# Three pairs' sums in attention and earlier slot conversions in a fused attention, MoE and gated-MLP kernel

## Chip, cores and metric

One Trainium2 chip, one core. The metric is the device time of one execution in microseconds (us), median of three runs; smaller is better.

## What is computed

```python
# q, k, v: [4, 8, 576, 64]; x: [2304, 512]; 8 experts 512 -> 1024 -> 512; then 512 -> 2048 -> 512, all float32
proj = x @ w_phi; proj -= max(abs(proj)); phi = concat(exp(proj), exp(-proj))
kv = sum_s phi(k) v;  z = sum_s phi(k)
attn = (phi(q) kv) / (phi(q) z + 1e-6)
# top-1 mixture of experts on the rows of attn
e = argmax(softmax(cosine(x, emb) / tau));  x = gate * (relu(x @ w1[e]) @ w2[e])
# gated layer
h = x @ w_in;  out = (h * sigmoid(h)) @ w_out
```

Every product is kept near float32 by splitting both operands into a high part (a rounded copy) and a low part (the rest) and adding three products: high by high, high by low and low by high. `w_in` and `w_out` arrive as 64-bit floats and are narrowed to 32 bits on the chip by integer operations.

## The kernel before

The order of work on every engine is the order of the program text; the engines run it in order, and an instruction that waits holds up all that stands behind it on its engine. So does the SyncE queue for DMAs and GpSimd's queue for its own DMAs and gathers.

**Attention** (0 to about 245 us). A loop over g = -2 to 31, one head of one batch each, about 6.5 us apiece. VectorE finds the maxima and subtracts them (L383, L384), ScalarE takes exponentials, GpSimd makes the low parts (`klow` L422, `low` L369), TensorE does the rest. Beside it, class `Convert` narrows 10 of the 16 blocks of `w_in`, numbers 4 to 13, two to a pair (pairs 2 to 6). One block costs four VectorE instructions (`narrow`: L194, L187 or L190, L199, L201). The dictionaries `CONV` and `BITS` say in which g a block is begun and two of its instructions run. Pairs 2 and 3 live in a region of eight 256-column pieces each; `SUMS` says in which g their sums are made (`sums`, L180 and twice L183: the gated layer's first product is done by a seven-product Strassen scheme, whose left operands are three plain pieces and four sums), after which one DMA stores pieces 1 to 7 in `sscr`. Of the other pairs only the four plain pieces are stored.

**Slots** (about 231 to 527 us). 22 slots of 128 tokens, each with one expert. In turn s of the loop TensorE does the first product of slot s in four blocks (`mm1(s, k)`, k = 0 to 3), transposes the rows of slot s+1 (`xturn`), does the second product of slot s-1 in four blocks (`mm2(s-1, i)`) and transposes the hidden rows of slot s (`hturn`). Behind `mm1(s, k)` ScalarE rounds a quarter of the next slot's weights into `wh` (L835) and VectorE makes the low part `wl` (L836); behind `mm2(s-1, i)` the same is done for the second weights of slot s. `xturn` ends with `xh` on ScalarE (L840) and `xl` on VectorE (L843), `hturn` with `hh` and `hl` on the same lines. In slots 1 to 8 VectorE also does the routing of the remaining slots in 13 bits (`route`, `PLAN`); the bit with the gate (L703) comes behind `mm1(4, 1)`, and ScalarE's L705 waits for it.

In the same loop six more blocks of `w_in` (J0 to J5) are narrowed in place, in a tile `x` of attention. `convert(s, n)` is called behind `mm1(s, n)` for n = 0 to 3 and behind `mm2(s-1, n-4)` for n = 4 to 7. `STEPS` lists the (s, n) at which one of the four parts of a block runs: part 1 on VectorE (L187 or L190), part 2 on VectorE (L209), part 3 on ScalarE (L212), part 4 on VectorE (L215). Each waits for the one before. `SLOTWORK` lists GpSimd's share: `cload` loads a raw block, `cplain` stores a narrowed one, `csum` and `cstore` make and store sums.

**Gated layer, first part** (about 524 to 711 us). 32 units of seven products each, about 0.8 us a product; unit u = 8k + q is token part k against pair q. `unit` runs the products in the order 1 of u, 5 of u, 4 of u-1, 6 of u, 3 of u-1, 2 of u, 7 of u. Behind products 1, 4, 6 and 7 ScalarE copies out (`keep`, L1110); behind 1, 3 and 2 VectorE joins (`join`, L1117), and SyncE stores the result. The join behind product 1 has to be done before product 3 of the same unit can write its bank. `at(u, n, f)` puts further work behind product n of unit u, in the order in which the text puts it there: weights (`wfetch`, `wsum`, `whigh`, `wlow`), inputs of the next part (`xsum`, `xsplit`), and the narrowing of `w_out`: `oload(j)` (SyncE, 512 KB), four times `owork(j)` (VectorE L194, L190, L199, L201), `ostore(j)` (SyncE). `oload` uses two buffers in turn, shared with `wfetch`.

```python
            for j, u in enumerate(units):
                at(u - 1, 4, oload, j)
            for j, u in enumerate(units):
                for n in (3, 3, 2, 2):
                    at(u, n, owork, j)
                at(u, 7, ostore, j)
```

**Gated layer, second part** (about 711 us to the end): 18 row tiles, TensorE throughout.

Of the kernel before, what the change touches and what calls it, by code (L numbers as in the profile page):

```python
# [12 lines left out]
I32 = mybir.dt.int32  # L13
# [21 lines left out]
NJP = NJ // 2  # L35
# [8 lines left out]
KWHOLE = 26  # L44
CA = 10
CT = 4
QD = 4
G = B * H
RK = 2
NXS = (2, 2, 2)  # L50
SQ = [{}, {1: (0, 1), 3: (2, 3), 5: (4,)}, {1: (0, 1), 3: (2, 3), 5: (4,)}, {i: (i,) for i in range(NB)}]
RANK = (1, 0)
WARM = (10, 14)
SUMS = {3: 0, 5: 0, 6: 0, 12: 1, 19: 1, 20: 1}
BITS = [-1, 0, 1, 2, 3, 4, 5, 6, 7, 11, 12, 13, 14, 15, 19, 20, 21, 22, 23, 24]
CONV = [-2, 0, 2, 4, 6, 11, 13, 15, 20, 22, 24]
ORDERED = {ET.PE, ET.Activation, ET.DVE, ET.SP}
# [12 lines left out]
def moe_kernel(ctx, tc, qk, v, w_phi, emb, tau, w1, w2, win, wout, out):  # L70
    nc = tc.nc
# [107 lines left out]
    def sums(r, eng):  # L179
        eng.tensor_tensor(out=r[:, 4:8:3], in0=r[:, 1:3], in1=r[:, 0:1].to_broadcast([P, 2, 256]), op=ALU.add)  # L180
        yield
        for o in (5, 6):
            eng.tensor_tensor(out=r[:, o], in0=r[:, o - 1], in1=r[:, o - 3], op=ALU.add)  # L183
# [33 lines left out]
    class Convert:  # L217
        def __init__(self, a, b):
            self.a, self.b, self.h, self.s = a, b, {}, {}

        def done(self, i):
            p, even = divmod(i, 2)
            o = 512 * (1 - even)
            return (self.b[:, p * 2048 + o:p * 2048 + o + 512] if p < 2 else self.a[:, 3072 + o:3584 + o]).bitcast(I32)

        def load(self, i):
            o = i % 3 * 1024
# [1 line left out]
            fetch_raw(i + CT, self.h[i])  # L229

        def step(self, k):
            if k > 4:
                keep_weights(k - 1 + CT, self.done(k - 1))
            if k + 2 < CA:
                self.load(k + 2)
            if k < CA:
                yield from narrow(self.h.pop(k), self.done(k), k)

        def pair(self, p):
            r = self.b[:, p * 2048:(p + 1) * 2048].rearrange("p (a f) -> p a f", a=8)  # L240
            yield from sums(r, nc.vector)
            yield
            nc.sync.dma_start(out=sscr[CT // 2 + p], in_=r[:, 1:8])

    def phase_all(ctx):
        x_ctx = ExitStack()
# [697 lines left out]
        def cplain(i):  # L944
            keep_weights(i + NJ - 2, J[i][0][:, 0:512], nc.gpsimd)

        SLOTWORK = {(3, 1): (cplain, 0), (4, 1): (cload, 2), (8, 3): (cplain, 1), (8, 7): (cload, 3),
                    (11, 1): (csum, 1), (13, 1): (cstore, 1), (13, 5): (cload, 4), (13, 7): (cload, 5),
                    (16, 1): (csum, 2), (16, 3): (cstore, 2)}
        STEPS = [(2, 1), (2, 3), (2, 5), (2, 7), (7, 1), (7, 5), (7, 7), (8, 1)]  # L950
        STEPS += [(s, n) for s in (9, 10, 14, 15) for n in (1, 3, 5, 7)]

        def convert(s, n):
# [13 lines left out]
        W = {}  # L967
# [14 lines left out]

        def wfetch(q):
            if q < QD:
                wspace(q)
                nc.sync.dma_start(out=W[q][1].bitcast(F32), in_=sscr[q].rearrange("p a f -> p (a f)"))
            else:
                W["r", q] = pools["ul"].tile([P, 2048], F32, tag="ws", name="ws", bufs=2)
                nc.sync.dma_start(out=W["r", q][:, 0:1024], in_=sscr[q].rearrange("p a f -> p (a f)"))
# [292 lines left out]
        project(1)  # L1282
        next(prep)
        cv = Convert(*(raw2[i].rearrange("p k f -> p (k f)") for i in (1, 0)))
        pairs = [cv.pair(p) for p in range(2)]
        first = None
        ch = [iter(())]
        cg = [iter(())]
# [9 lines left out]
        for g in range(-2, G):  # L1298
            b, h = divmod(g, H)
            for u in (3, 4) if g == -2 else (g + 6,):  # L1300
                if u < G:
                    load_qk(u)
            if g == -2:
                cv.load(0)
                cv.load(1)
            if h == 4 and b + 1 < B and g > 0:
                start_batch(b + 1)
            if 2 <= g + 3 < G:
                project(g + 3)
            if 1 <= g + 3 < G:  # L1310
                shift(g + 3)
            if g == G - 1:
                split(1, 1, 2)
            if 0 <= g + 1 < G:
                kv_turn(g + 1)
            if g == -2:
                next(prep, None)
            if g >= 0:
                numden(g)
                norm(g)  # L1320
            if g == G - 1:
                choose_all(B - 1)
                xstore(B - 1)
            nx(4)
            if g == G - H + 3:
                next(rest_of_ranks, None)
            if g in SUMS:
                next(pairs[SUMS[g]], None)
            if g in BITS:
                nv(2)  # L1330
            if g >= H and h == 0:
                xstore(b - 1)
            if g in (G - H + 4, G - H + 6):
                load2((g - G + H - 4) // 2)
            if g == G - 3:
                xturn(0)
            if 0 <= g + 2 < G:
                qturn(g + 2)
            if g == -2:
                high(2)  # L1340
                low(2, nc.vector)
            if KWHOLE <= g + 3 < G:
                kwhole(g + 3)
            if 0 <= g + 3 < KWHOLE:
                vhigh(g + 3)
                vlow(g + 3)
            if 1 <= g + 3 < KWHOLE:
                kexp(g + 3, 0)
                kround(g + 3, 0)
                klow(g + 3, 0)  # L1350
                kexp(g + 3, 1)
            if 0 <= g + 2 < G:
                kv_part(g + 2)
            if g >= H and h == (0 if g >= G - H else RK):
                ranks(b - 1, beside(g + 2))
                if g == G - H:
                    rest_of_ranks = rank_rest()
                    next(rest_of_ranks)
            if g == G - H + 1:
                first = route_first(r1)  # L1360
                next(first)
                next(rest_of_ranks)
            if 0 <= g + 2 < G:
                kv_copy(g + 2)
            for u in () if g == -2 else (3, 4) if g == -1 else (g + 5,):
                if u < G:
                    load_v(u)
            if g == G - H + 3:
                next(first)
                gather(0)  # L1370
                gather(1)
            if 1 <= g + 3 < KWHOLE:
                kround(g + 3, 1)
                klow(g + 3, 1)
            if 0 <= g + 2 < G:
                qexp(g + 2)
            if g + 5 < G:
                high(g + 5)
                low(g + 5, nc.gpsimd)
            if g >= H:  # L1380
                for c in SQ[b].get(h, ()):
                    squares(b - 1, c, 0, 0, DM)
            if g == G - H + 2:
                nv(9)
                next(first)
                next(rest_of_ranks)
            if g in CONV:
                nv(9)
                cg[0] = cv.step(CONV.index(g))
                if g == CONV[-1]:  # L1390
                    nv(9)
            if g in (G - H + 1, G - H + 3):
                load1((g - G + H) // 2)
            if g == G - 4:
                att2.close()
                open_pools("early")
                split(0, 1, 0)
            if g == G - 3:
                split(0, 1, 1)
                split(0, 1, 2)  # L1400
                mm1(0, 0)
                for c in range(NB):
                    squares(B - 1, c, 0, 0, DM - 2 * D)
            if g == G - 2:
                mm1(0, 1)
                gather(2)
                split(0, 1, 3)
                split(1, 1, 0)
                mm1(0, 2)
                split(1, 1, 1)  # L1410
            if h == H - 1 and g > 0:
                if g == G - H - 1:
                    choose_all(b)
                elif g < G - 1:
                    ch[0] = choose(b)
# [114 lines left out]
        for q in range(4, NJP):  # L1530
            wspace(q)
        FR = wside(NJP - 2, 1), wside(NJP - 1, 0), wside(NJP - 1, 1, F32)
        wfetch(4)
        wfetch(5)
        def plan():
            for q in (2, 3):
                at(q - 2, 6, whigh, q)
                at(q - 1, 5 if q == 2 else 1, wlow, q)
            for q in range(4, NJP):
                at(q - 2, 1, wsum, q)  # L1540
                at(q - 2, 2, whigh, q)
                at(q - 1, 1, wlow, q)
            at(3, 5, wfetch, 6)
            at(4, 5, wfetch, 7)
            at(0, 2, xscale, 1, 0)
            at(1, 2, xscale, 1, 1)
            for k in range(1, NT // (2 * TN)):
# [8 lines left out]
                at(u + 5, 2, xsum, k, "T1n")  # L1556
                at(u + 6, 1, xsum, k, "T2n")
                at(u + 6, 6, xsum, k, "T3")
                at(u + 6, 2, xsum, k, "T4")
                for v, n, name in ((7, 5, "T1n"), (7, 6, "T2n"), (7, 2, "B21"), (7, 7, "T3"), (8, 4, "T4"), (8, 3, "B22")):  # L1560
                    at(u + v, n, xsplit, k, name)
            units = [u for u in range(6, 25) if u not in (7, 15, 23)]
            assert len(units) == NJ
            for j, u in enumerate(units):
                at(u - 1, 4, oload, j)
            for j, u in enumerate(units):
                for n in (3, 3, 2, 2):
                    at(u, n, owork, j)
                at(u, 7, ostore, j)
            for m in range(4):  # L1570
                at(26 + m, 1, ofetch, 2 * m)
                at(26 + m, 6, ofetch, 2 * m + 1)
# [69 lines left out]
```

## Time and profile before

| what | value |
|---|---|
| time, median of 3 runs | 923.54 us (922.74 to 923.62) |
| the profiled execution's own time | 924.59 us |
| its span in the profile | 922.9 us |
| TensorE busy | 900.4 us, 98% |
| VectorE, ScalarE, GpSimd busy | 636.8, 582.3, 243.0 us |

The span is what the instructions of the program cover; 1.7 us of the profiled execution's time lie around it. Busy shares are means over four stages with different limits. A busy TensorE is not TensorE at its peak; its idle time in the timeline is what the text goes by.

### The profile page before, as it was taken

Reading aid. Unit: us, or ns where it says so; the run is one execution under the profiler, and the core shown is the slowest. Engines: PE = TensorE matmul, PEld = TensorE weight load, DVE = VectorE, ACT = ScalarE, POOL = GpSimd, SP = SyncE. Lnnn points to the kernel's source line nnn. Section 1 sums busy time; section 2 is a strip of 40 time slices with the busy share of each in tenths; the row PEclk is TensorE's granted clock in tenths of the full one; section 3 lists DMA queues with packets and bytes.
Section 4 is the critical chain, followed back from the end, with each engine's and each line's share of the span. In section 5 each row is a group of like instructions: output and inputs, shape, how many; then the busy total and the mean of one; then the engine's idle time right before and its main releaser. Section 6 shows DMA issues by size and latency. Waiting matters only on the chain. (4 is left out here: it accounts for less than half of the span.)

```text
span 922.9 us, 15620 instructions
## 1 busy us (share of the span) xinstructions
PE 900.4 (98%) x5567; PEld 785.7 (85%) x5567; DVE 636.8 (69%) x982; ACT 582.3 (63%) x948; POOL 243.0 (26%) x221
## 2 busy tenths in 40 slices
PE   8999999999999999999999999999999999999996
PEld 5999999997777787878888799999999888888884
DVE  7899898987698999969989778575755222222220
ACT  6867878745876979869889665343455444333331
POOL 6887888812101402410500020101000100000000
PEclk9999999999999999999999999999999999999998
DMA  6355354339455724791497555778786744444410
GB/s 181 95 151 152 93 153 122 102 105 343 163 201 179 271 109 149 254 378 59 157 355 274 197 195 189 235 256 237 237 260 219 191 114 114 117 122 123 124 40 23
DMA packets 127330, 162.37 MB, mean 176 GB/s; under 512 B 34184, under 2 KB 88072, under 8 KB 127248
## 3 DMA queue, kind: packets, MB, share of 16 engines
q1 hardware_dynamic: 121136, 141.30, 48.6%
q0 software_dynamic: 6032, 19.99, 6.3%
q8 instruction: 45, 0.74, 0.3%
q14 instruction: 37, 0.30, 0.1%
q10 hardware_dynamic: 80, 0.03, 0.0%
HBM read 163.14 MB, written 44.30 MB: 225 GB/s over the span
## 5 line engine op out<-in xcount | busy, mean ns | idle before, releaser
L836 DVE TENSOR_TENSOR wl<-raw,wh 128x1024 fp32r<-128x1024 f32 (+1 forms) x166 | 190.6, 1193 | 25.2 <-ACT wh L835 20.2
L835 ACT CAST wh<-raw 128x1024 fp32r<-128x1024 f32 (+1 forms) x166 | 161.2, 1032 | 20.9 <-DMA raw<-w 11.4
L1187 DVE TENSOR_TENSOR hlt<-gt,hlt 128x1024 fp32r<-128x1024 f32 x34 | 41.7, 1226 | 146.4 <-ACT hlt L1186 146.4
L787 PE MATMUL po<-wob,hlt 128*128 128x512 f32 x272 | 108.5, 399 | 0.0
L786 PE MATMUL po<-wob,hlt 128*128 128x512 f32 x272 | 107.2, 394 | 0.0
L1110 ACT COPY ht<-puA 128x288 f32<-128x288 f32 x128 | 50.8, 400 | 88.8 <-PE puA L788 76.7
L788 PE MATMUL po<-wob,hlt 128*128 128x512 f32 x272 | 106.6, 392 | 0.0
L422 POOL TENSOR_TENSOR kl<-ke,kh 128x640 fp32r<-128x640 f32 x52 | 85.3, 1662 | 31.2 <-issue 23.8
L1207 ACT COPY os<-po 128x512 f32<-128x512 f32 x17 | 10.0, 588 | 108.2 <-PE po L788 108.2
L472 PE MATMUL pnx<-kv,qp 128*128 128x73 f32 x640 | 76.6, 275 | 0.0
L472 PEld LDWEIGHTS pnx<-kv,qp 128*128 128x128 f32 x640 | 74.1, 192 | 0.1
L786 PE MATMUL ph<-wh,xh 128*128 128x512 f32 x166 | 67.1, 404 | 0.0
L788 PE MATMUL ph<-wh,xl 128*128 128x512 f32 x166 | 65.2, 393 | 1.2 <-DVE xl L843 1.2
L787 PE MATMUL ph<-wl,xh 128*128 128x512 f32 x166 | 64.8, 390 | 0.0
L1208 POOL DMA_INDIRECT out<-os,oidx x18 | 17.6, 976 | 179.1 <-ACT os L1207 168.6
L407 ACT ACTIVATE ke<-d 128x640 f32<-128x640 f32 x52 | 38.3, 737 | 38.2 <-DVE d L384 38.2
L786 PEld LDWEIGHTS po<-wob,hlt 128*128 128x128 f32 x272 | 51.1, 188 | 13.2
L788 PEld LDWEIGHTS po<-wob,hlt 128*128 128x128 f32 x272 | 51.1, 188 | 12.3
L787 PEld LDWEIGHTS po<-wob,hlt 128*128 128x128 f32 x272 | 51.1, 188 | 11.8
L1117 DVE TENSOR_TENSOR ht<-puC,ht 128x288 f32<-128x288 f32 x64 | 29.1, 454 | 46.0 <-PE puC L788 38.4
L377 PE MATMUL pqk<-wbd,zh 128*128 128x256 f32 (+1 forms) x320 | 59.3, 284 | 0.8 <-DVE d L384 0.6
L1019 POOL DMA_INDIRECT yt<-yd,yidx x13 | 15.2, 1166 | 166.1 <-PE pt L1036 153.9
(406 smaller groups left out, 2461.6 us busy)
## 6 DMA issues: line engine op xcount, KB each, us to landing
raw<-w SPq DMA_DIRECT2D x44, 1536.0 KB
raw<-w SPq DMA_DIRECT2D x44, 512.0 KB
hd<-ht SPq DMA_DIRECT2D x124, 144.0 KB
gt<-hd SPq DMA_DIRECT2D x15, 1024.0 KB
z<-qk SPq DMA_DIRECT2D x32, 288.0 KB
wo<-wout SPq DMA_DIRECT2D x16, 512.0 KB
yd<-ys SPq DMA_DIRECT2D x23, 256.0 KB
raw<-win SPq DMA_DIRECT2D x10, 512.0 KB
```

Source lines behind the costliest of these rows:

```text
L377: nc.tensor.matmul(out=pqk[0:r, c * 256:(c + 1) * 256], lhsT=z[:, c * P:c * P + r], rhs=wbd[:, j].rearrange("p h f -> p (h f)"), start=(i ...
L407: nc.scalar.activation(out=ke, in_=kd, func=AF.Exp, scale=1.0 - 2.0 * s)
L422: nc.gpsimd.tensor_tensor(out=kl[:, :, s, :], in0=st.pop(("ke", g, s)), in1=kh[:, :, s, :].bitcast(F32), op=ALU.subtract)
L472: nc.tensor.matmul(out=pn[:, c, 0:73], lhsT=qp[:, s, c * P:(c + 1) * P], rhs=kv[:, s, 0:73], start=(s == 0), stop=(s == 1))
L786: nc.tensor.matmul(out=o, lhsT=ah, rhs=bh, start=first, stop=False, skip_group_check=more)
L787: nc.tensor.matmul(out=o, lhsT=ah, rhs=bl, start=False, stop=False, skip_group_check=more)
L788: nc.tensor.matmul(out=o, lhsT=al, rhs=bh, start=False, stop=last, skip_group_check=more)
L835: nc.scalar.copy(out=hi[:, 0:n], in_=sl[:, 0:n])
L836: nc.vector.tensor_tensor(out=lo[:, 0:n], in0=sl[:, 0:n], in1=hi[:, 0:n].bitcast(F32), op=ALU.subtract)
L1110: nc.scalar.copy(out=htile(u, at), in_=BK[u, "A"])
L1117: nc.vector.tensor_tensor(out=o, in0=BK[u, b], in1=o, op=ALU.add)
L1187: nc.vector.tensor_tensor(out=lo, in0=g, in1=hi.bitcast(F32), op=ALU.subtract)
```

## The change

Four things are changed together.

1. In attention a third pair (number 4) gets its sums there. Its blocks are narrowed into the region of the first pair, once that is stored. Each of the three pairs is stored in three pieces (pieces 1 to 3, 4 and 5, 6 and 7) at the g that `KEEP` names, instead of in one DMA. The second part of the second pair's sums moves from g = 19 to 14. `QD` is 5: pair 4 is then fetched whole and not summed in unit 2; `wfetch(6)` moves from unit 3 to the start.
2. The parts of slot block J0 move from slot 2 to slots 1 and 2, those of J1 from slots 7 and 8 to slots 2 and 3. Their stores move to slot 6, the loads of J2 and J3 to slot 7. The parts of J2 to J5 stay in slots 9, 10, 14 and 15.
3. In the gated layer `owork` moves from behind products 3 and 2 to behind products 1 and 5, `oload` from behind product 4 to behind product 5, `ostore` from behind product 7 to behind product 3.
4. The sum T4 for token part 1 moves from behind product 2 of unit 6 to behind product 1 of unit 7.

```diff
-QD = 4
+QD = 5
-SUMS = {3: 0, 5: 0, 6: 0, 12: 1, 19: 1, 20: 1}
+SUMS = {3: (0, 1), 5: (0, 2), 12: (1, 1), 14: (1, 2), 19: (2, 1), 23: (2, 2)}
+KEEP = {4: (0, 1, 4), 6: (0, 4, 6), 8: (0, 6, 8), 9: (1, 1, 4), 16: (1, 4, 6), 17: (1, 6, 8), 18: (2, 1, 4), 24: (2, 4, 6),
+        25: (2, 6, 8)}
...
+        def region(self, p):
+            return self.b[:, p % 2 * 2048:(p % 2 + 1) * 2048]
+
         def done(self, i):
             p, even = divmod(i, 2)
             o = 512 * (1 - even)
-            return (self.b[:, p * 2048 + o:p * 2048 + o + 512] if p < 2 else self.a[:, 3072 + o:3584 + o]).bitcast(I32)
+            return (self.a[:, 3072 + o:3584 + o] if p > 2 else self.region(p)[:, o:o + 512]).bitcast(I32)
...
         def step(self, k):
-            if k > 4:
+            if k > 6:
                 keep_weights(k - 1 + CT, self.done(k - 1))
...
-        def pair(self, p):
-            r = self.b[:, p * 2048:(p + 1) * 2048].rearrange("p (a f) -> p a f", a=8)
-            yield from sums(r, nc.vector)
-            yield
-            nc.sync.dma_start(out=sscr[CT // 2 + p], in_=r[:, 1:8])
+        def sum(self, p, n):
+            if n == 1:
+                self.s[p] = sums(self.region(p).rearrange("p (a f) -> p a f", a=8), nc.vector)
+            next(self.s[p], None)
+
+        def keep(self, p, a, b):
+            nc.sync.dma_start(out=sscr[CT // 2 + p][:, a - 1:b - 1], in_=self.region(p)[:, 256 * a:256 * b].rearrange(
+                "p (a f) -> p a f", a=b - a))
...
-        SLOTWORK = {(3, 1): (cplain, 0), (4, 1): (cload, 2), (8, 3): (cplain, 1), (8, 7): (cload, 3),
+        SLOTWORK = {(6, 1): (cplain, 0), (6, 3): (cplain, 1), (7, 1): (cload, 2), (7, 3): (cload, 3),
...
-        STEPS = [(2, 1), (2, 3), (2, 5), (2, 7), (7, 1), (7, 5), (7, 7), (8, 1)]
+        STEPS = [(1, 3), (1, 7), (2, 1), (2, 2), (2, 3), (2, 5), (2, 7), (3, 5)]
...
             if g in SUMS:
-                next(pairs[SUMS[g]], None)
+                cv.sum(*SUMS[g])
+            if g in KEEP:
+                cv.keep(*KEEP[g])
...
-        wfetch(4)
-        wfetch(5)
+        for q in (4, 5, 6):
+            wfetch(q)
         def plan():
-            for q in (2, 3):
+            for q in range(2, QD):
                 at(q - 2, 6, whigh, q)
                 at(q - 1, 5 if q == 2 else 1, wlow, q)
-            for q in range(4, NJP):
+            for q in range(QD, NJP):
...
-            at(3, 5, wfetch, 6)
             at(4, 5, wfetch, 7)
...
-                at(u + 6, 2, xsum, k, "T4")
+                at(u + 7 if k == 1 else u + 6, 1 if k == 1 else 2, xsum, k, "T4")
...
-                at(u - 1, 4, oload, j)
+                at(u - 1, 5, oload, j)
             for j, u in enumerate(units):
-                for n in (3, 3, 2, 2):
+                for n in (1, 1, 5, 5):
                     at(u, n, owork, j)
-                at(u, 7, ostore, j)
+                at(u, 3, ostore, j)
```

## Rows read from the trace of the kernel before

**Rows 1.** The page, part 1: busy us, share of the span, instructions.

```profile
PE 900.4 (98%) x5567; PEld 785.7 (85%) x5567; DVE 636.8 (69%) x982; ACT 582.3 (63%) x948; POOL 243.0 (26%) x221
```

**Rows 2.** Timeline of TensorE: start, length, work, [idle before it <- releaser].

```profile
168.09 0.67 PE L460 MATMUL pkv<-ie,kvt 65*128 65x73 f32 x4 [0.38 <-ACT kvt L453]
...
259.78 0.50 PE L788 MATMUL ph<-wh,xl 128*128 128x512 f32 x1 [0.40 <-DVE xl L843]
...
312.54 0.50 PE L788 MATMUL ph<-wh,xl 128*128 128x512 f32 x1 [0.37 <-DVE xl L843]
...
408.36 0.50 PE L786 MATMUL py<-wh,hh 128*128 128x512 f32 x1 [1.57 <-ACT hh L840]
...
561.50 0.40 PE L786 MATMUL puA<-xcT,wbr 128*128 128x288 f32 x1 [0.33 <-ACT ht L1110]
...
616.65 0.40 PE L786 MATMUL puC<-xcB,wbr 128*128 128x288 f32 x1 [0.61 <-DVE ht L1117]
```

**Rows 3.** Windows: length, busy (count) of PE, PEld, DVE, ACT, POOL; clock, DMA.

```profile
249.00:292.00 43.00, 42.60 (x200) 30.54 (x199) 41.87 (x87) 31.48 (x47) 6.46 (x8) 1.00 0.58 202
295.00:312.00 17.00, 17.00 (x79) 12.74 (x77) 16.12 (x22) 17.00 (x26) 5.03 (x4) 1.00 0.69 255
313.00:345.00 32.00, 32.00 (x170) 25.94 (x169) 31.27 (x46) 23.10 (x34) 3.84 (x2) 1.00 0.41 148
```

**Rows 4.** Timeline of VectorE in slots 2 to 4.

```profile
268.90 0.42 DVE L187 TENSOR_SCALAR x<-x 128x512 int32<-128x512 int32 x1
...
270.37 0.68 DVE L209 SCALAR_TENSOR_TENSOR x<-x 128x512 int32<-128x512 int32 x1
...
276.35 0.70 DVE L215 SCALAR_TENSOR_TENSOR x<-x 128x512 int32<-128x512 int32 x1
276.95 1.02 DVE L843 TENSOR_TENSOR hl<-ht,hh 128x512 fp32r<-128x512 f32 x2
277.88 1.22 DVE L836 TENSOR_TENSOR wl<-raw,wh 128x1024 fp32r<-128x1024 f32 x1
...
291.96 0.17 DVE L703 TENSOR_TENSOR gate<-ssq 128x20 f32<-128x20 f32 x1
```

**Rows 5.** Timeline of ScalarE in slots 2 to 4.

```profile
271.09 0.70 ACT L212 ACTIVATE x<-x 128x512 f32<-128x512 f32 x1 [2.61 <-DVE x L209]
271.68 1.03 ACT L835 CAST wh<-raw 128x1024 fp32r<-128x1024 f32 x1
272.62 0.85 ACT L840 CAST hh<-ht 128x512 fp32r<-128x512 f32 x2
...
274.10 2.96 ACT L835 CAST wh<-raw 128x1024 fp32r<-128x1024 f32 x3
...
292.16 0.22 ACT L705 ACTIVATE gate<-gate 128x20 f32<-128x20 f32 x1 [2.60 <-DVE gate L703]
...
296.15 1.07 ACT L876 ACTIVATE hs<-ph 128x512 f32<-128x512 f32 x2
```

**Rows 6.** Timeline of VectorE and GpSimd in attention, g = 14 and g = 19.

```profile
124.38 0.42 DVE L194 TENSOR_SCALAR raw<-raw 128x512 f32<-128x512 f32 x1
...
125.05 3.08 POOL L422 TENSOR_TENSOR kl<-ke,kh 128x640 fp32r<-128x640 f32 x2 [1.03 <-issue]
...
158.35 0.87 DVE L183 TENSOR_TENSOR raw<-raw 128x256 f32<-128x256 f32 x2
159.14 1.79 DVE L194 TENSOR_SCALAR raw<-raw 128x512 f32<-128x512 f32 x1
```

**Rows 7.** Timeline of SyncE's queue and of VectorE in units 13 to 15.

```profile
607.70 0.33 SPq L172 DMA_DIRECT2D wo<-wout  x1
...
613.10 0.43 DVE L194 TENSOR_SCALAR wo<-wo 128x512 f32<-128x512 f32 x1 [1.33 <-DMA wo<-wout]
...
615.53 0.69 DVE L201 SCALAR_TENSOR_TENSOR wo<-wo 128x512 int32<-128x512 int32 x1
616.14 0.45 DVE L1117 TENSOR_TENSOR ht<-puC,ht 128x288 f32<-128x288 f32 x1
```

More of the change, by code (lines that the diff above doesn't have):

```diff
@@ L984, in wfetch @@
             if q < QD:
-                wspace(q)
+                if q not in W:
+                    wspace(q)
                 nc.sync.dma_start(out=W[q][1].bitcast(F32), in_=sscr[q].rearrange("p a f -> p (a f)"))
@@ L1284, in phase_all @@
         cv = Convert(*(raw2[i].rearrange("p k f -> p (k f)") for i in (1, 0)))
-        pairs = [cv.pair(p) for p in range(2)]
         first = None
```

## The prediction

> **What bounds the kernel now.** The page comes first: TensorE is busy for 98% of the span, the next engine for 69% [rows 1]. So time can only be won where TensorE is idle, and an edit costs something only where it makes TensorE idle. The timeline of TensorE says where that is, one sort of gap after the other [rows 2]: 0.38 us in attention, released by a copy on ScalarE; 0.40 and 0.37 us in the slots, both released by `xl` on VectorE; 1.57 us for slot weights; 0.33 us in unit 5 of the gated layer, behind a ScalarE copy; 0.61 us in unit 15, released by a `join` on VectorE. Third, the windows of the slots [rows 3]. From 249 to 292 us VectorE is busy 41.87 of 43 us, and what is missing are the seams between short instructions: it has no pause at all. From 295 to 312 ScalarE is busy 17.00 of 17 us, VectorE 16.12. TensorE's gap at 312.54 is the end of that backlog. From 313 to 345 VectorE is as full, 31.27 of 32, but TensorE is busy 32.00: there it does not feel VectorE.
>
> **Attention.** Removed from SyncE: two 256 KB stores and two whole-pair stores; added: nine pieces. All are issued a head or more after their data is made, behind loads that run several heads ahead, and nothing waits for them but a region's reuse two heads later: 0 us. Added on VectorE: one pair's three sum instructions; taken from unit 2, where no gap is listed: 0 us there. What counts is which narrowing instruction they push. L194 took 0.42 us at 124.38, where it was done before GpSimd's `kl` began at 125.05, and 1.79 us at 159.14, behind the two L183 (0.87 us), alongside `kl` [rows 6]. At g = 14 the pair of L183 now comes before the first of these, so both its narrowing instructions run late and slow, some 0.8 + 2 x 1.37 = 3.5 us more on VectorE; that is the work of g = 19 before, and that was followed by the gap at 168.09 of 0.38 us [rows 2]. In return g = 19 loses it: its L180 stands where g = 12 had one. At g = 23 the head begun is the 26th, for which the text makes no `kl`, so the narrowing stays fast and the sums cost their own 0.8 us of VectorE. Sum 0, one gap for the other; bounds -0.4 (g = 19 relieved, the rest hidden) and +0.8 (a gap at 14 and one at 23).
>
> **Slots: the vector parts.** A row of VectorE begins some 0.08 us before the one ahead ends; so part 1 (0.42) takes 0.34, part 4 0.60 (276.35 to 276.95), and part 2, nearly as long, the same [rows 4]. Part 1 of J0 now stands ahead of `xl` of slot 2, for which TensorE already waits at 259.78 [rows 2]: 0.34 us at once. By `hl` of slot 2 (276.95) VectorE had done three parts, 1.54 us; now it does five, 2.48: 0.94 more. Part 4 of J1 behind `mm2(2, 1)` adds 0.60. These 1.54 us go into a stretch with no pause [rows 3], ahead of the gate (L703 at 291.96), for which ScalarE stood idle 2.60 us [rows 5]; behind it ScalarE and VectorE are full to 312. So they arrive at the gap at 312.54 whole.
>
> **Slots: ScalarE's part.** Part 3 of J1 now stands at (2, 7), and ScalarE's queue behind it holds `hh` of slot 2, the output copy and the rounding of slot 4's first weights. It waits for part 2 at (2, 5), which VectorE reaches only about 276.1: the place of part 4 before, 276.35, less one `wl` (1.22 - 0.08 = 1.14), plus 0.94. Before, part 3 stood behind `mm2(1, 1)`: it waited too, 2.61 us, but was over at 271.09, and `hh` came at 272.62, 4.3 us before VectorE wanted it [rows 4, 5]. Now, from the end of part 2: ScalarE needs 0.59 for part 3 (271.09 to 271.68), 1.48 for `hh` and copies (272.62 to 274.10), 1.03 for one rounding: 3.1 us. VectorE meanwhile has one `wl` (1.14) and the two `hl` (0.93): 2.1. Then it stands 1.0 us, some 1.2 with its own end of part 2 (0.08) and the hand-overs (0.04 from L209's end at 271.05 to L212), before the `wl` for slot 4 (277.88 before). The lower bound is 0 (part 2 earlier than I place it), the upper 1.4 (`hl` waits for `hh` too). The delay at L703 is 0.94 + 1.2 + 0.60 = 2.7 us. ScalarE's next copies, `hs` of slot 4 at 296.15, move with it, and so does `xl` of slot 6. **Slots: +2.7**, bounds 1.5 and 3.2. It comes in three gaps: 0.3 at slot 2, the rest at slots 4 to 6.
>
> What J1 frees in slots 7 and 8 is worth 0: TensorE has no gap from 313 to 345 [rows 3]. GpSimd no longer waits for J1's end with gathers behind it; no gap of TensorE was released by a gather. Two stores and two loads, 1.5 MB, move into the stretch around 320 us, where the DMA share is 0.41 [rows 3] and no gap of TensorE was released by a load. 0.
>
> **Gated layer.** TensorE's 0.61 us in unit 15 come from a `join` at 616.14, which stood behind four `owork`, of which the first waited 1.33 us for its load (issued 607.70, used 613.10: 5.4 us) [rows 7]. Moved to products 1 and 5, `owork` no longer stands just ahead of that join; its last two, 0.6 each as L201 shows, alone are twice the gap. I give 0.5 of the 0.61, since the load can still be late. Between units 6 and 7 the order is the same, with T4 besides, but no gap is listed there: 0.1. The gap in unit 5 stays: `whigh(7)` waits for `wsum(7)` as before. Fetching pair 4 whole adds 384 KB to a start at which nothing waits for it: 0. The shorter lead of `oload` (six products, 4.8 us, instead of nine, 7.2) lets VectorE stand 5.4 - 4.8 = 0.6 us or more at the head of some units, but the join that TensorE needs is ahead of `owork` in the queue. **Gated layer: -0.6**, bounds -1.0 (both gaps, 0.61 and 0.33) and +0.6 (one such stand reaches TensorE).
>
> The row that bears on that lead is the 512 KB load with at most 5.4 us [rows 7]. The Trainium skill, DMA: Bandwidth & Descriptors, section Anatomy of one DMA (for GpSimd's path), gives a DMA a fixed part of about 2 us and a part of bytes by 436 GB/s: by estimate 3.2 us here. By that the load would always be in time and the gated layer would give -1.0, the sum +1.7; the trace, with 5.4, has the load slower. The same fixed part speaks against storing in pieces: five more DMAs would be some 10 us by that page, if anything waited for them.
>
> **Sum.** 2.7 + 0 - 0.6 = +2.1 us. The profiled execution took 924.59, 1.05 above the median; 926.7 by its own time, **925.6** by the median.
>
> **Rivals.** *The delay does not reach TensorE whole (0.31).* Only the 1.5 us of vector parts count, or the weights' gap of 1.57 at 408.36 [rows 2] swallows part of the shift; and the gated layer gives 1.0. +0.5 us, 924.0. For it: the ScalarE wait hangs on where VectorE is to within 1 us. Against the swallowing: the loads of that stretch are released by TensorE and would move too. *The load of `w_out` becomes the wait (0.10).* Should loads land over 6 us after their issue, VectorE stands at the head of most units, late enough for the next head join; 16 units at 0.15 us: -0.6 turns into +1.8, 928.0. *Slots 7 and 8 pay (0.07).* If TensorE is paced by VectorE from 313 to 345, so that J1's 1.54 us and ScalarE's 0.70 come off there, and the early parts hide, it gives -1.5 - 0.6: 921.4. It decides if TensorE's spacing there is wider than elsewhere; the window, TensorE 32.00 of 32 busy, shows no gap, which is why the chance is small.
>
> **Chances.** 0.2% of 923.54 is 1.85 us, about what a measurement here can tell from no change. My forecast has 0.52, of which 0.11 falls under 1.85, since its sum is so near to it. Slower: 0.41 + 0.10 + 0.02 of the first rival = 0.53. Same: 0.11 + 0.29 = 0.40. Faster: 0.07. Range: downward the first rival's 924.0 with attention's -0.4, 923.6; upward the upper bounds of slots and gated layer, 3.2 + 0.6, 927.3. The forecast's own: 2.7 - 1.0 - 0.4 = +1.3 to 3.2 - 0.2 = +3.0, 924.8 to 926.5.
>
> **What would show it.** Right: L212 with an idle of some 5 us before it near 277; `wl` behind `hl` of slot 2 waiting about 1 us for `wh`; L703 2 to 3 us later; TensorE gaps at `xl` of slots 2, 4 and 6 and before `ht` of slot 4 with the sum 2 to 3 us larger; the slots' end as much later; the join of unit 15 earlier, VectorE waiting for `wo` more often. Attention should end within half a us of where it did. Wrong: L703 moved by under 1 us, or a gap at 408 that is gone, or a gated layer that is longer.

## The result, and the profile after

The changed kernel takes 931.15 us (median of 4, 930.99 to 932.42), the kernel before, run beside it, 923.58: a ratio of 1.0083, interval 1.0065 to 1.0100. That is 7.6 us slower; the prediction was +2.1, and 927.3 at the upper end. The profiled execution's span went from 922.9 to 929.5 us, +6.6. The other 1.0 us is that the profiled execution of before (924.59 us) lay 1.0 us above the median; 0.9 of that is one gap in unit 15, which most other executions do not have (experiment 3).

First the page of the changed kernel, part 1, beside [rows 1]: TensorE's busy time is 2.2 us more, its share a point less.

```profile
PE 902.6 (97%) x5567; PEld 786.0 (85%) x5567; DVE 641.9 (69%) x982; ACT 582.7 (63%) x948; POOL 239.4 (26%) x221
```

The timeline of TensorE in the changed kernel (line numbers are 8 or 9 higher in this part of the code than before: L788 is L796, L840 is L848, L1117 is L1126), the rows at which it was late:

```profile
134.15 0.33 PE L468 MATMUL pkv<-ie,kvt 65*128 65x73 f32 x1 [0.39 <-ACT kvt L461]
148.67 0.44 PE L468 MATMUL pkv<-ie,kvt 65*128 65x73 f32 x2 [0.39 <-ACT kvt L461]
...
169.17 0.34 PE L468 MATMUL pkv<-ie,kvt 65*128 65x73 f32 x2
197.74 0.33 PE L468 MATMUL pkv<-ie,kvt 65*128 65x73 f32 x1 [0.92 <-ACT kvt L461]
262.22 0.50 PE L796 MATMUL ph<-wh,xl 128*128 128x512 f32 x1 [0.68 <-DVE xl L851]
317.45 0.50 PE L796 MATMUL ph<-wh,xl 128*128 128x512 f32 x1 [1.18 <-DVE xl L851]
337.75 0.50 PE L794 MATMUL py<-wh,hh 128*128 128x512 f32 x1 [1.35 <-ACT hh L848]
345.67 0.40 PE L794 MATMUL ph<-wh,xh 128*128 128x512 f32 x1
413.51 0.47 PE L794 MATMUL py<-wh,hh 128*128 128x512 f32 x1
566.41 0.40 PE L794 MATMUL puA<-xcT,wbr 128*128 128x288 f32 x1 [0.23 <-ACT ht L1119]
572.67 0.40 PE L794 MATMUL puC<-xcT1n,wbr 128*128 128x288 f32 x1 [1.23 <-DVE ht L1126]
620.90 0.40 PE L794 MATMUL puC<-xcT1n,wbr 128*128 128x288 f32 x1 [1.24 <-DVE ht L1126]
623.39 0.29 PE L794 MATMUL puC<-xcB,wbr 128*128 128x288 f32 x1
```

The way to read them is to lay the start of one matmul in both traces side by side. The four that need a row of before beyond [rows 2]:

```profile
195.72 0.45 PE L460 MATMUL pkv<-ie,kvt 65*128 65x73 f32 x3
...
331.25 0.47 PE L786 MATMUL py<-wh,hh 128*128 128x512 f32 x1
...
338.56 0.39 PE L786 MATMUL ph<-wh,xh 128*128 128x512 f32 x1
...
566.36 0.30 PE L786 MATMUL puC<-xcT1n,wbr 128*128 128x288 f32 x1
```

| matmul, before | after | later by | what lies between |
|---|---|---|---|
| 168.09 | 169.17 | 1.08 | g = 14: +1.7; the gap of g = 19 gone: -0.6 |
| 195.72 | 197.74 | 2.02 | g = 23: +0.9 |
| 259.78 | 262.22 | 2.44 | `xl` of slot 2 |
| 312.54 | 317.45 | 4.91 | `xl`, `hs`, `xl` of slots 3 to 6 |
| 331.25, 338.56 | 337.75, 345.67 | 6.50, 7.11 | `hh`, `hl` of slot 7: weights late |
| 408.36 | 413.51 | 5.15 | the gap for weights is gone |
| 561.50 | 566.41 | 4.91 | |
| 566.36 | 572.67 | 6.31 | unit 7 |
| 616.65 | 623.39 | 6.74 | unit 15 |

So, against this one execution of before, attention gave +2.0, the slots +2.9, +2.2 and -2.2 (0.3 of it just behind 408.36), the gated layer +1.8.

**Attention.** VectorE and GpSimd of the changed kernel at g = 14, then at g = 23:

```profile
124.40 0.87 DVE L185 TENSOR_TENSOR raw<-raw 128x256 f32<-128x256 f32 x2
125.19 1.80 DVE L196 TENSOR_SCALAR raw<-raw 128x512 f32<-128x512 f32 x1
126.91 1.78 DVE L189 TENSOR_SCALAR raw<-raw 128x512 int32<-128x512 int32 x1
128.61 1.48 DVE L391 TENSOR_REDUCE m<-pqk 128x10 f32<-128x1280 f32 x1
...
125.07 3.33 POOL L430 TENSOR_TENSOR kl<-ke,kh 128x640 fp32r<-128x640 f32 x2 [1.04 <-issue]
...
189.81 1.40 POOL L377 TENSOR_TENSOR zl<-z,zh 128x576 fp32r<-128x576 f32 x1 [4.12 <-ACT zh L371]
...
189.83 1.44 DVE L510 TENSOR_TENSOR oh<-em8c,mx 128x40 bf16<-128x40 f32 x1
```

The same maximum in the kernel before, and two later places where VectorE waits, the next one and the first behind g = 19:

```profile
126.86 1.49 DVE L383 TENSOR_REDUCE m<-pqk 128x10 f32<-128x1280 f32 x1 [1.72 <-PE pqk L377]
...
152.41 0.20 DVE L539 TENSOR_TENSOR rk<-pkv,oh 128x40 f32<-128x40 f32 x1 [0.60 <-PE pkv L535]
...
175.09 1.49 DVE L383 TENSOR_REDUCE m<-pqk 128x10 f32<-128x1280 f32 x1 [0.99 <-PE pqk L377]
```

Both narrowing instructions are slow, as forecast: 0.8 + 2 x 1.37 = 3.5 us. 1.72 of it went into VectorE's wait; the other 1.75 is the distance from 126.86 to 128.61. From there to 152.41 VectorE has no pause, so all of it reaches TensorE, in three steps (0.8, 0.5 and 0.4 us, the last at 148.67). At g = 23 the narrowing stays fast, as forecast, but the 0.8 us of sums push the small L510, 0.20 us before, behind the start of GpSimd's `zl` (189.81): 1.44. The second narrowing instruction ends at 128.69, 0.29 us behind GpSimd's two `kl` (125.07 + 3.33), L510 at 191.27, 0.06 behind `zl`. The Trainium skill, SBUF — State Buffer, section Who interferes with whom, has the rule: VectorE and GpSimd share one pair of ports, and of two instructions that both need it the one that starts first holds it for its whole length, while the other stands still. The trace agrees, with 1.80, 1.78 and 1.44 us in place of 0.42, 0.42 and 0.20.

**Slots.** ScalarE and VectorE of the changed kernel:

```profile
278.97 0.69 ACT L214 ACTIVATE x<-x 128x512 f32<-128x512 f32 x1 [6.49 <-DVE x L211]
...
336.59 0.62 ACT L843 CAST wh<-raw 128x512 fp32r<-128x512 f32 x1 [7.43 <-DMA raw<-w]
...
282.14 1.23 DVE L844 TENSOR_TENSOR wl<-raw,wh 128x1024 fp32r<-128x1024 f32 x1 [0.96 <-ACT wh L843]
...
296.82 0.22 DVE L711 TENSOR_TENSOR gate<-ssq 128x20 f32<-128x20 f32 x1
```

L711 is 4.86 us behind L703 of [rows 4], 2.02 of it from attention: 2.84, where 2.7 was forecast, with the wait of ScalarE (6.49, forecast some 5) and of `wl` (0.96, forecast about 1). What was not forecast is the second row. In the kernel before it read

```profile
326.14 0.62 ACT L835 CAST wh<-raw 128x512 fp32r<-128x512 f32 x1 [1.88 <-DMA raw<-w]
```

**Gated layer.** VectorE of the changed kernel in units 6 and 14:

```profile
568.70 0.75 DVE L1070 SCALAR_TENSOR_TENSOR xf<-xf 128x576 f32<-128x576 f32 x1
569.37 0.42 DVE L196 TENSOR_SCALAR wo<-wo 128x512 f32<-128x512 f32 x1
569.70 0.42 DVE L192 TENSOR_SCALAR wo<-wo 128x512 int32<-128x512 int32 x1
570.16 0.69 DVE L201 SCALAR_TENSOR_TENSOR wo<-wo 128x512 int32<-128x512 int32 x1
570.88 0.69 DVE L203 SCALAR_TENSOR_TENSOR wo<-wo 128x512 int32<-128x512 int32 x1
571.50 0.75 DVE L1066 TENSOR_TENSOR xf<-xf 128x576 f32<-128x576 f32 x1
572.16 0.45 DVE L1126 TENSOR_TENSOR ht<-puC,ht 128x288 f32<-128x288 f32 x1
...
617.59 0.43 DVE L196 TENSOR_SCALAR wo<-wo 128x512 f32<-128x512 f32 x1 [2.05 <-DMA wo<-wout]
...
619.73 0.75 DVE L1066 TENSOR_TENSOR xf<-xf 128x576 f32<-128x576 f32 x1
620.39 0.45 DVE L1126 TENSOR_TENSOR ht<-puC,ht 128x288 f32<-128x288 f32 x1
```

Products 1 and 5 follow each other, so four `owork` stand in a row. Behind them come T3 (L1066) and the join behind product 3 of the unit before. Product 5 of the next unit writes the same bank and waits for it: 572.67 and 620.90 on TensorE. In unit 6 VectorE had no pause; in unit 14 it also waited 2.05 us for the load, issued at 612.26: SyncE had waited for the store out of the same buffer, which landed at 612.25.

### The profile page after: what moved, and what is told of

Its sections match the earlier page's. It is cut to its first block, busy times and chain, and to the rows that moved or that the text cites. A ratio compares the mean times of both kernels' runs of the same rounds, so it can differ in the third digit from the quotient of the medians.

```text
span 929.5 us, 15606 instructions
## 1 busy us (share of the span) xinstructions
PE 902.6 (97%) x5567; PEld 786.0 (85%) x5567; DVE 641.9 (69%) x982; ACT 582.7 (63%) x948; POOL 239.4 (26%) x221
## 5 line engine op out<-in xcount | busy, mean ns | idle before, releaser
L796 PE MATMUL po<-wob,hlt 128*128 128x512 f32 x272 | 106.6, 392 | 0.0
L796 PE MATMUL ph<-wh,xl 128*128 128x512 f32 x166 | 65.6, 395 | 2.5 <-DVE xl L851 2.5
L796 PEld LDWEIGHTS po<-wob,hlt 128*128 128x128 f32 x272 | 51.0, 188 | 12.3
L391 DVE TENSOR_REDUCE m<-pqk 128x10 f32<-128x1280 f32 x32 | 47.4, 1483 | 13.9 <-PE pqk L385 13.9
```

The lines of the kernel that those rows point to most:

```text
L391: nc.vector.tensor_reduce(out=m, in_=pv, axis=AX.X, op=ALU.max, apply_absolute_value=True)
L796: nc.tensor.matmul(out=o, lhsT=al, rhs=bh, start=False, stop=last, skip_group_check=more)
```

## The experiments

Times are medians with the ratio to the kernel before, run beside them (923.7 to 923.9 us), and its 95% interval. Single executions of one kernel spread by some 3 us, so the traces say where, the ratios whether.

**1. The attention part alone.** The kernel before with the hunks of `SUMS`, `KEEP`, `Convert`, `QD` and `wfetch`:

```diff
-QD = 4
+QD = 5
-SUMS = {3: 0, 5: 0, 6: 0, 12: 1, 19: 1, 20: 1}
+SUMS = {3: (0, 1), 5: (0, 2), 12: (1, 1), 14: (1, 2), 19: (2, 1), 23: (2, 2)}
```

> The kernel before with part 1 of the change alone (sums of three pairs, stores in pieces, pair 4 fetched whole). Theory: TensorE's matmuls stand 2.0 us later at the end of attention, as in the changed kernel, because an instruction pushed against GpSimd's work at g = 14 and at g = 23 takes 1.4 us longer each and VectorE has no pause there; everything behind moves along, weights and transfers too, so 923.6 + 2.0 = 925.6 us. Rival 1: the gap of 1.57 us at 408 us swallows the shift, 923.6 to 924.1 us. Rival 2, the prediction: the attention part costs nothing, 923.6 us, with no later end of attention.

Measured: 926.82 us, 1.0033 (1.0022 to 1.0044). TensorE is 1.8 us late at 147, 1.2 at 168, 2.1 at 196 us, as in the changed kernel; the gap at 408 us shrank from 1.57 to 1.24 us only. The prediction's 0 falls. The profiled execution also lost 1.8 us between 198 and 203 us to the clock (last section); so the median's +3.1 holds more than the 2.1 us of gaps.

**2. The slots part alone.** The hunks of `SLOTWORK` and `STEPS`:

```diff
-        STEPS = [(2, 1), (2, 3), (2, 5), (2, 7), (7, 1), (7, 5), (7, 7), (8, 1)]
+        STEPS = [(1, 3), (1, 7), (2, 1), (2, 2), (2, 3), (2, 5), (2, 7), (3, 5)]
```

> The kernel before with part 2 of the change alone (the parts of J0 and J1 earlier, their stores and loads in slots 6 and 7). Theory: some 2.9 us of gaps at xl and hs of slots 2 to 6, then 2.2 us at hh of slot 7, where the weights land late behind two stores and two loads issued within 7 us, and 2.3 us given back at the gap of 408 us, which closes: +2.8, 926.4 us. Rival 1: the gap at 408 us closes only because attention shifted too; then it stays and the sum is +5.1, 928.7 us. Rival 2, the prediction: +2.7 from the vector and scalar work alone, 926.3 us, with no gap at hh of slot 7 and the gap at 408 us kept.

Measured: 926.08 us, 1.0034 (1.0020 to 1.0047). By the trace +2.9 at 315 us, then 0.7 for the late weights (2.2 with the whole change), and 2.2 back at 408 us, where no gap is left: rival 1 falls. The 2.9 are the prediction's term. The time alone, 926.1, would also fit the prediction's 926.3; that, against the prediction, weights are late at slot 7 and the gap at 408 us is gone, only the trace shows.

**3. The gated-layer part alone.** The hunks of `oload`, `owork`, `ostore` and T4:

```diff
-                for n in (3, 3, 2, 2):
+                for n in (1, 1, 5, 5):
```

> The kernel before with parts 3 and 4 of the change alone (owork behind products 1 and 5, oload and ostore with it, T4 of token part 1 moved). Theory: four owork in a row stand ahead of the join behind product 3 of the unit before, for which product 5 of the next unit waits; TensorE stands 1.4 us in units 7 and 15 instead of 0.3 and 0.8: +1.9, 925.5 us. Rival, the prediction: that join is ahead of owork, -0.6, 923.0 us, with no gap of over 0.3 us in units 7 and 15.

Measured: 926.40 us, 1.0026 (1.0015 to 1.0038), +2.7; the trace has +1.9 behind unit 15. The prediction's sign is refuted.

The 0.8 us between the two are the gap of 0.61 us in unit 15 that the trace of before has (616.65, [rows 2]). Eight of the profiled executions have the gated layer as it was: before and experiments 1, 2, 5, 6, 8, 9 and 11. Only two of them have that gap, before and experiment 6 (0.88 us), the two in which VectorE stood over a microsecond for the load of unit 14 (1.33 and 1.55 us). In the others it stood at most 0.64 us, as here in experiment 2, and TensorE has no such gap and comes through the unit 0.6 to 0.9 us sooner:

```profile
613.47 0.43 DVE L194 TENSOR_SCALAR wo<-wo 128x512 f32<-128x512 f32 x1 [0.50 <-DMA wo<-wout]
```

So in most of these executions there was nothing to win in unit 15; against them the changed gated layer costs 2.7 us.

**4. The stores and loads back at their places,** in the changed kernel:

```diff
-        SLOTWORK = {(6, 1): (cplain, 0), (6, 3): (cplain, 1), (7, 1): (cload, 2), (7, 3): (cload, 3),
+        SLOTWORK = {(3, 1): (cplain, 0), (4, 1): (cload, 2), (8, 3): (cplain, 1), (8, 7): (cload, 3),
```

> The changed kernel with the stores of J0 and J1 and the loads of J2 and J3 at their former places (slots 3, 4 and 8), the parts staying in slots 1 to 3. Theory: the weights of slot 7 land in time, the gap of 1.6 + 0.6 us at hh and hl of slot 7 is gone; if the gap at 408 us stays closed, 931.2 - 2.2 = 929.0 us. Rival 1: the gap is not from these transfers and stays: 931.2 us. Rival 2: the gap at slot 7 goes, but the weights' gap at 408 us comes back in its place: 930.5 to 931.3 us.

Measured: 929.78 us, 1.0060 (1.0046 to 1.0075), 1.4 less than the changed kernel; by the traces, leaving out what this execution lost to the clock near 200 us, 2.3 less behind slot 7. ScalarE in this kernel:

```profile
332.43 0.62 ACT L843 CAST wh<-raw 128x512 fp32r<-128x512 f32 x1 [1.99 <-DMA raw<-w]
```

The wait is 1.99 in place of 7.43 us, and TensorE's two gaps at slot 7 are gone; the one at 408 us did not come back. So the four transfers, issued between 317.7 and 324.8 us, were what delayed the weights.

**5. The sums at other heads,** in the attention part alone:

```diff
-SUMS = {... 14: (1, 2), 19: (2, 1), 23: (2, 2)}
+SUMS = {... 18: (1, 2), 19: (2, 1), 25: (2, 2)}
```

> The attention part alone, as in the first experiment (926.8 us, TensorE 2.0 us later behind g = 23 without counting its clock), with the second sums of pair 3 at g = 18 instead of 14 and of pair 4 at g = 25 instead of 23, where VectorE was idle before (1.43 us at 154.27, 1.21 us at 201.29), and their stores 2 to 4 heads later. Theory: the cost was the place, where a pushed instruction starts next to GpSimd's; the gaps at 133, 148 and 196 us go, the relief at g = 19 stays: attention ends 0 to 0.6 us earlier than before, time 923.2 to 924.4 us. Rival: 0.8 us of sums cost that much anywhere in attention, so two of them leave 0.8 to 1.6 us: 924.8 to 925.5 us.

The stores that `KEEP` names move along. Measured: 922.57 us, 0.9996 (0.9987 to 1.0006), against 926.82. TensorE stands 0.8 us earlier than before from 168 us on. VectorE at g = 14 has its wait again, and L510 its 0.20 us:

```profile
126.63 1.49 DVE L391 TENSOR_REDUCE m<-pqk 128x10 f32<-128x1280 f32 x1 [1.70 <-PE pqk L385]
...
187.13 0.20 DVE L510 TENSOR_TENSOR oh<-em8c,mx 128x40 bf16<-128x40 f32 x1
```

The same sums cost nothing there: it was the place, not the work.

**6. The narrowing ahead of the sums,** in every head of the attention part:

```diff
+            if g in BITS:
+                nv(2)
             if g in SUMS:
                 cv.sum(*SUMS[g])
...
-            if g in BITS:
-                nv(2)
```

> The attention part alone, with the two narrowing instructions of a head ahead of the sums instead of behind them, in every head. Theory: any such VectorE instruction that starts after GpSimd's kl has begun waits until that one has ended, so now a sum instruction waits 1.4 us in place of the narrowing; the gaps of g = 14 stay (0.5 us each at 133 and 148 us) and the time is that of the first experiment, 926.3 to 927.3 us. Rival: only the narrowing instructions, with one operand, are held up; done early they take 0.42 us, the sums 0.42 us each, the gaps of g = 14 go and the time is about 1.7 us lower, 925.1 us.

Measured: 924.03 us, 1.0007 (0.9998 to 1.0016). Both theories missed:

```profile
123.39 0.42 DVE L196 TENSOR_SCALAR raw<-raw 128x512 f32<-128x512 f32 x1
123.73 0.42 DVE L189 TENSOR_SCALAR raw<-raw 128x512 int32<-128x512 int32 x1
124.06 2.14 DVE L185 TENSOR_TENSOR raw<-raw 128x256 f32<-128x256 f32 x2
126.12 1.48 DVE L391 TENSOR_REDUCE m<-pqk 128x10 f32<-128x1280 f32 x1
```

A sum does wait as well: 2.14 us for two that take 0.87, so the rival falls. But now three of the four instructions had begun before GpSimd's `kl` (124.07), and one wait is left of two: at g = 14 TensorE loses 0.1 us in place of 1.6. The theory expected one wait in exchange for another; what counts is how many VectorE instructions are still to begin when `kl` begins. The gap of 0.39 us at 72 us went in the same way, and TensorE stands 0.8 us earlier from there on; the one at 168 us had gone in experiment 1 already. The gap of g = 23 (0.92 us at 195.29) stayed, since L510 is pushed all the same.

**7. `owork` of units 6 and 14 alone back,** in the gated-layer part alone:

```diff
-                for n in (1, 1, 5, 5):
+                for n in (3, 3, 2, 2) if u in (6, 14) else (1, 1, 5, 5):
                     at(u, n, owork, j)
-                at(u, 3, ostore, j)
+                at(u, 7 if u in (6, 14) else 3, ostore, j)
```

> The gated-layer part alone (926.4 us), with owork of units 6 and 14 alone back behind products 3 and 2 and their ostore behind product 7. Theory: four owork in a row ahead of T3 and of the join behind product 3 are the cost, in these two units, where VectorE has a sum each before and after; TensorE's gap in unit 7 falls from 1.4 to at most 0.3 us, in unit 15 from 1.4 to 0.8: 924.7 us. Rival: the shorter lead of the load is the cost in all units; then gaps remain there or appear in other units, and the time stays at 926.4 us.

Measured: 923.26 us, 0.9992 (0.9983 to 1.0001), 3.1 less than with all units moved; no gap over 0.2 us in units 7 and 15. Two of the 16 places were the whole cost. That it fell below the forecast 924.7 is the gap of unit 15 again: the 0.8 us that were to stay there did not come. In this trace the later loads cost nothing.

**8. J0 alone early,** in the kernel before:

```diff
-        STEPS = [(2, 1), (2, 3), (2, 5), (2, 7), (7, 1), (7, 5), (7, 7), (8, 1)]
+        STEPS = [(1, 3), (1, 7), (2, 1), (2, 2), (7, 1), (7, 5), (7, 7), (8, 1)]
```

> The kernel before with the parts of J0 alone early (slots 1 and 2), those of J1, all stores and loads where they were. Theory: J1 is the whole cost of the slots; here VectorE has no more work ahead of the gate than before, so the gap at xl of slot 2 grows by 0.35 us and the one of slot 6 shrinks by as much: 923.7 us, and the weights' gap at 408 us stays at 1.4 to 1.8 us since VectorE still narrows J1 in slots 7 and 8. Rival: work ahead of hl of slot 2 costs 0.94 us at once and is not given back: 924.6 us or more.

Measured: 923.84 us, 1.0000 (0.9990 to 1.0011). The gap at `xl` of slot 2 grows by 0.3, the one of slot 6 shrinks by as much, the one at 408 us stays (1.60). J1 is the cost.

**9. Part 3 of J1 later,** stores and loads as before:

```diff
-        STEPS = [(2, 1), (2, 3), (2, 5), (2, 7), (7, 1), (7, 5), (7, 7), (8, 1)]
+        STEPS = [(1, 3), (1, 7), (2, 1), (2, 2), (2, 3), (2, 5), (3, 1), (3, 5)]
```

> The kernel before with the parts of J0 and J1 early as in the change, but part 3 of J1 (ScalarE) at (3, 1) instead of (2, 7); stores and loads at their former places. Theory: ScalarE no longer stands for part 2, so of the 2.9 us by which the slots part alone delayed TensorE up to 317 us the 1.2 us of ScalarE's wait go and 1.5 to 1.7 us of VectorE's work stay; no late weights at 331 us; the gap of 1.8 us at 408 us closes because VectorE and ScalarE have no parts in slots 7 and 8: 923.5 us. Rival 1: ScalarE's wait costs nothing and 2.9 us stay: 924.8 us. Rival 2: the gap at 408 us needs the transfers of the change to close and stays: 925.2 us or more.

Measured: 922.95 us, 0.9991 (0.9982 to 1.0000).

```profile
276.98 0.69 ACT L212 ACTIVATE x<-x 128x512 f32<-128x512 f32 x1 [0.84 <-DVE x L209]
```

ScalarE waits 0.84 us in place of 6.49. TensorE is 1.64 us late at 314.18, not 2.9: VectorE's work was put at 1.54, ScalarE's wait at 1.2. The gap at 408 us is gone with the transfers where they were, so it closes because J1's parts left slots 7 and 8.

**10. Two parts mended:** the changed kernel with the slots as before and the edits of experiments 5 and 7.

> The changed kernel with the slots as before, the two second sums of attention at g = 18 and 25, and owork of units 6 and 14 behind products 3 and 2. Theory: the two mends add up, 1.1 us and 0.4 us under the kernel before by their medians, 0.8 and 0.9 us by TensorE's positions in their traces: 921.9 to 922.2 us. Rival: what is gained ahead of 408 us is lost there, where the weights set the time: 923.0 to 923.7 us.

Measured: 922.59 us, 0.9986 (0.9977 to 0.9995), between theory and rival. The gap at 408 us is there (1.32), and one of 0.69 us at 601.31, where VectorE had stood 3.91 us until the load of `w_out` landed, 6.75 us after its issue: the shorter lead can cost something after all.

**11. The loads of J4 and J5 a slot later.**

```diff
-                    (11, 1): (csum, 1), (13, 1): (cstore, 1), (13, 5): (cload, 4), (13, 7): (cload, 5),
+                    (11, 1): (csum, 1), (13, 1): (cstore, 1), (14, 3): (cload, 4), (14, 7): (cload, 5),
```

> The kernel before with the loads of J4 and J5 in slot 14 instead of 13, and their parts, sums and stores one slot later. Theory: the weights that TensorE waits for at 408 us are late because four stores and these two loads share the DMA engines with them; with the loads behind, the gap falls from 1.8 us to at most 0.5 us: 922.2 us. Rival: the gap moves to the next slot whose weights share with them, 923.7 us.

Measured: 927.82 us, 1.0048 (1.0034 to 1.0061), and it says nothing about the theory: GpSimd's queue issued the two loads at 398.07 and 399.61 us as before (398.36, 399.94), since nothing in it holds them back until slot 14. The gap was longer, not shorter (2.87), and the clock fell behind it; why it grew was not followed up.

**12. All mended:** experiment 10 with the steps of experiment 9.

> The kernel with two parts mended (922.6 us) and the slots' parts as in the experiment with part 3 later, stores and loads at their former places. Theory: the parts leave 1.6 us of gaps up to 317 us and close the gap of 1.6 + 0.3 us at 408 us, since without J1 in slots 7 and 8 the weights' loads are issued 1.3 to 1.9 us earlier relative to TensorE: 0 to 0.6 us less than 922.6, 922.0 to 922.6 us. Rival: the loads move with TensorE as in the attention part alone, the gap at 408 us stays, and the time is 924.2 us.

Measured: 922.03 us, 0.9979 (0.9971 to 0.9988), as the theory has it: 1.8 us less than the kernel before and 9 less than the changed one; no gap at 408 us.

## Why the prediction was wrong

| term | forecast | in the traces | shown by |
|---|---|---|---|
| attention | 0 (-0.4 to +0.8) | +2.0 | experiments 1, 5, 6 |
| slots: J1's parts up to the gap of slot 6 | +2.7 | +2.9 | 2, 8, 9 |
| slots: stores and loads | 0 | +2.2 | 4 |
| slots 7 and 8 freed | 0 | -2.2 | 8, 9 |
| gated layer | -0.6 (-1.0 to +0.6) | +1.8 | 3, 7 |
| sum | +2.1 | +6.7 | |

The gated layer's +1.8 is counted against the one execution of before that has the gap of unit 15. Against executions without it the term is +2.7, the median of experiment 3, and the sum 7.6, as measured.

- **Attention: the step that failed is the price.** It worked out VectorE's 3.5 us at g = 14, then priced them by the gap after g = 19, 0.38. Behind g = 19 VectorE pauses again at 175.09 (0.99 us), some 13 us after the maximum that follows its narrowing (162.54); behind g = 14 it has no pause for 25 us. The chain of rows was there: a wait of 1.72, then nothing until 152.41. The work cost 1.7 us there. Less the 0.6 won at g = 19, that is +1.1. At g = 23 it looked only at the narrowing for GpSimd's company; the small instruction behind was pushed into it, +0.9.
- **Slots, J1's parts: right in mechanism and size,** down to the two waits. Experiment 9 separates the two portions, 1.6 and 1.3 against 1.54 and 1.2. That the slots as a whole, +2.9, also come near the forecast +2.7 is luck: two terms that were put at 0, +2.2 and -2.2, cancel.
- **Slots, transfers: "no gap of TensorE was released by a load" was the failing step.** It describes the stretch before, where the DMA share was 0.41 [rows 3]. With four transfers added next to the weights it became 0.69 (313 to 345 us), and the weights' last piece came 10.45 us later, 326.14 to 336.59, on a TensorE 4.9 us late.
- **Slots 7 and 8: worth 2.2, not 0,** though not where the rival looked. TensorE has no gap there; without J1, the weights of slot 12 are issued no later than before while TensorE is later (experiment 9: the four loads from 385.88, before from 386.20; with J1 there, in experiment 1, they move with TensorE, to 390.02), and land 1.7 us sooner. ScalarE before and in experiment 9:

```profile
407.20 0.62 ACT L835 CAST wh<-raw 128x512 fp32r<-128x512 f32 x1 [6.19 <-DMA raw<-w]
...
405.49 0.62 ACT L835 CAST wh<-raw 128x512 fp32r<-128x512 f32 x1 [4.45 <-DMA raw<-w]
```

  Part of the rival "the delay does not reach TensorE whole", the swallowing at 408, came true by this. Why the load itself is quicker was not found.
- **Gated layer: "the join that TensorE needs is ahead of `owork` in the queue" is wrong.** It holds for the join behind product 1. Product 5 of the next unit needs the one behind product 3, which stands behind. The 0.5 us that the prediction hoped to win in unit 15 came from a gap that two of eight executions have. The rival with the load as the wait has a share, 2.05 us of VectorE's time in unit 14 and the gap in experiment 10.

Part 4, T4, ran only together with part 3; experiment 7, which has both, shows no gain beyond its interval, and what part 4 gives alone is not shown.

## What to carry to other kernels

Price extra work on a busy engine by the distance to that engine's next pause, not by a gap that similar work left elsewhere: the same 0.8 us of sums cost 1.7 and 0.9 us at two heads and nothing at two others. A gap that a change is to win back should first be looked for in a second execution: the one of unit 15 is in two of eight. When work is put behind another instruction, list each wait of the bottleneck that is now behind it, one bank and one product at a time. And a place without a wait for loads says nothing of how many transfers it can take.

## What the runs showed of the hardware

In experiment 1's profile TensorE's granted clock was halved for some 3 us, from 199.8 us on, 2 us behind the end of the gap of 0.92 us at g = 23 (197.83); between the two TensorE was busy throughout. Windows of this kernel: length, busy time and count of PE, PEld, DVE, ACT, POOL, then clock, DMA share, GB/s:

```profile
198.00:199.00 1.00, 1.00 (x11) 1.00 (x11) 0.97 (x3) 1.00 (x3) 0.00 (x0) 1.00 1.14 301
199.00:200.00 1.00, 1.00 (x11) 1.00 (x10) 0.96 (x2) 1.00 (x3) 0.50 (x1) 0.91 0.65 170
200.00:201.00 1.00, 1.00 (x6) 1.00 (x6) 1.00 (x1) 0.04 (x1) 0.90 (x1) 0.50 0.89 342
201.00:202.00 1.00, 1.00 (x7) 1.00 (x7) 0.93 (x5) 0.60 (x1) 0.00 (x0) 0.50 0.02 6
```

0.50 is the lower of its two levels, 1.2 of 2.4 GHz; 6 and 7 matmuls in a microsecond stand where 11 stood. It cost 1.8 us. Four profiled executions have this gap of 0.92 us: in experiments 1 and 4 the clock fell behind it, in the changed kernel and experiment 6 it kept 1.00. In none of the ten executions without the gap did it fall near there. What decides between the two outcomes is not shown. Experiment 11 has the same fall 1.3 us behind the start of the matmul that ended its gap of 2.87 us. Such falls may be one source of the 3 us by which single executions spread: in experiment 5 the two longest, 924.75 and 925.84 us, have a mean granted clock of 0.995, the others 0.996 to 0.998.
